# Results of one attention unit and scores of the next in one visit, with the seven products of a step in another order on four banks

## The chip, the cores and the metric

The kernel runs on one core of a Trainium2 chip. The metric is the device time of one execution in microseconds (us), the median of three runs. The engines are TensorE (PE, matrix products; its weight loads are listed as PEld), VectorE (DVE), ScalarE (ACT), GpSimd (POOL) and SyncE (SP, which here only issues DMAs). Products land in PSUM, which has eight banks; a tile of 128 x 512 fp32 fills one. DVE and ACT read PSUM, POOL doesn't.

## The reference, cut to what matters

```python
def reference(q, k, v, moe_w_in, moe_w_out, moe2_w_in, moe2_w_out, moe2_g_ln):
    # retention with a state: batch 4, 8 heads, 768 positions, head size 64
    for t in range(768):
        state = gamma * state + einsum('bhd,bhe->bhde', k[:, :, t], v[:, :, t])
        y[:, :, t] = scale * einsum('bhd,bhde->bhe', q[:, :, t], state)
    x = y.transpose(0, 2, 1, 3).reshape(3072, 512)
    h = x @ moe_w_in                        # 512 -> 2048
    x = (h - tanh(h)) @ moe_w_out           # 2048 -> 512
    h = x @ moe2_w_in                       # 512 -> 1024
    # softmax-weighted h, layer norm with moe2_g_ln, @ moe2_w_out -> 512
```

All is float32. The kernel keeps float32 accuracy by splitting each factor of a large product into a high and a low part and adding three products (high by high, high by low, low by high).

## The kernel before, in words

The attention is cut into units k: 128 positions of one batch, 24 units in all, 16 of them (k = 0 to 15) done in earlier stages. A unit has two parts, both in `unit` (L285). The **scores** (tiles `sc`, 64 small matmuls of 64 x 64 into two banks) are masked on DVE (L337) and make the running states `sb` and `sa` (L342, L345). The **results** (tiles `out`, 64 small matmuls into two banks) use the masked scores and the state; ACT copies a half (L317) and DVE adds the other (L319) into `xf`. `prepare` (L258) scales the input of a unit ahead of its scores, on POOL (L268, L279) and ACT (L275); `load_units` issues the loads of `z`.

The diff touches the stage of **h by seven** (from `ps_h` at L790 to `A.close()`), in which h of the positions 256 to 767 is computed with seven products in place of eight (a Strassen-Winograd scheme). In one step n a block of columns j is treated for a pair p of position blocks: seven products P1 to P7, each of six wide matmuls (128 x 128 by 128 x 512, L818) into one bank. There are 16 steps: n = 0 to 7 for the pair whose input is ready, n = 8 to 15 for the last pair, whose input `xf` comes out of the eight remaining units (k = 16 to 23, called 0 to 7 in `visits`) while steps 0 to 7 run.

Per step: P1(n) goes into bank b1 (`begin`, run in step n - 1) and ACT copies it (`keep`, L828, tile `part`). P2 goes into b3, and DVE adds the copy of P1 (`summed`, L844, tile `hs`). P5 goes into b2 and is copied. P6 is added onto b1 and copied (`u2`). P7 is added onto b1; DVE adds P5's copy. P4 is added onto b1 a step later; P3 is added onto b2 a step later, and DVE adds u2. Four results leave a step through `finish`: tanh on ACT (L834), then h - tanh (L836), on POOL after P2, P3 and P7 and on DVE after P4, then a store `gd` on SP. In steps 1 to 6 a `Factors` object makes the parts of the weights of step n + 1: four sums on DVE (L591 to L594), high parts (`cast`, L610, ACT), low parts (`low`, L614, DVE).

In steps 3 to 8 the input of the last pair is made: `late_x` (`sum_at`, L895 to L901, DVE) subtracts halves of `xf` from each other, and `put_x` (`x_at`) splits one of seven inputs into a high part (L171, ACT, 128 x 1024) and a low part (L172, DVE).

The order: in this stage PE's instructions stand in the order of the code (`manual_schedule`), and `late[0]` is set, so those of ACT, DVE and POOL keep the order of the code among themselves too (`fix`, `pin`). A planner orders only SP's DMAs. Before, the order of the products on PE in a step is P2, P5, P4 (of n - 1), P6, P3 (of n - 1), P1 (of n + 1), P7. `visit(n, m)` is called behind some of the products and runs the scores or the results of a unit there, as `visits` says. The pool `ps_h` has six banks that all of b1, b2 and b3 take in turn; `ps_a` has two banks, for the visits. Behind the stage comes y, the product with the second weights, on four banks from `y_banks`, with the first matmuls of y already in the last step.

Of the kernel before, what the change touches and what calls it, by code (L numbers as in the profile page):

```python
# [26 lines left out]
F32 = mybir.dt.float32  # L27
# [64 lines left out]
def body(ctx: ExitStack, tc, z, w_in, w_out, w_in2, w_out2, g_ln, cst, tab, out):  # L92
# [83 lines left out]
    class Decoder:  # L176
# [24 lines left out]
        def keep(self, fixed=False):  # L201
            while unkept:
                i, wf = unkept.pop(0)
                to = wfd[i % NJ1][:, i // NJ1, :] if i < NF1 else wod[i - NF1]
                eng = nc.gpsimd if i < NF1 else nc.scalar
                pin(eng.dma_start(out=to, in_=wf), fixed)
# [421 lines left out]
    def store_w():  # L628
        while made:
            j, parts_ = made.pop()  # L630
            if j >= NJ1 - 2:
                continue
            for i, u in enumerate(parts_):
                n = 3 if i < 2 else 4
                nc.sync.dma_start(out=wcd[j][i][:, :n, :], in_=u[:, :n, :].bitcast(F32))
# [145 lines left out]
    for b in range(2):  # L781
# [5 lines left out]
    M = ExitStack()  # L787
    M.enter_context(tc.manual_schedule(engines={mybir.EngineType.PE}))
    G = ExitStack()
    ps_h = G.enter_context(tc.tile_pool(name="ps_h", bufs=6, space=PSUM, reuse_waits="tile"))  # L790
    ps_a = G.enter_context(tc.tile_pool(name="ps_a", bufs=2, space=PSUM, reuse_waits="tile"))
    visits = {
        (0, P2): ("sc", 0), (0, P6): ("out", 0), (0, P7): ("sc", 1),
        (1, P5): ("out", 1), (1, P6): ("sc", 2), (1, P7): ("out", 2),
    }
    for k in range(3, 8):
        visits[k - 1, P5] = ("sc", k)
        visits[k - 1, P7] = ("out", k)

    def visit(n, m):  # L800
        if (n, m) not in visits:
            return
        kind, k = visits[n, m]
        k += 4 * B
        if kind == "sc":
            unit(None, k, pool=ps_a)
            load_units(k + 3)
            if k + 1 < NU:
                prepare(k + 1, H // 2, True, False)
        else:  # L810
            unit(k, None, opool=ps_a)

    def product(left, p, m, ph, first=True):
        n = 0
        for i in range(2):
            (ah, al), (xh, xl) = ([t[:, i, :] for t in side] for side in (left[m], xs[p, m]))
            for a, x in ((ah, xh), (ah, xl), (al, xh)):
                nc.tensor.matmul(  # L818
                    ph, a, x, start=first and n == 0, stop=n == 5, skip_group_check=True
                )  # L820
                n += 1

    def bank():
        return ps_h.tile([P, SB], F32, tag="h", name="ph")

    def keep(ph):
        t = t2([P, SB], F32, "part")
# [26 lines left out]
    py = []  # L854

    def y_banks(s):
        at = [(ps_h, "h")] * 4 if s % 2 else [(ps_a, "r"), (ps_a, "r"), (ps_h, "h"), (ps_h, "h")]
        py[:] = [pool.tile([P, SB], F32, tag=tag, name="py") for pool, tag in at]

    def load_g(upto):  # L860
# [19 lines left out]
    def split_wo(f):  # L880
        wo[f] = stage3(wof[f], None, nc.vector, late[0])

    def begin(n):
        b1[n] = bank()
        product(wl[n], q[n][0], P1, b1[n])
        p1[n] = keep(b1[n])

# [16 lines left out]
        (3, P3): P1, (4, P3): P2, (NJ1 - 1, P5): P5, (NJ1 - 1, P6): P6,  # L904
        (NJ1, P2): P7, (NJ1, P6): P4, (NJ1, P7): P3,
    }
    sum_at = {(5, P3): 0, (NJ1 - 1, P2): 1, (NJ1 - 1, P4): 2, (NJ1, P5): 3}

    def after(n, m):
        if (n, m) in sum_at:  # L910
            late_x(sum_at[n, m])
        if (n, m) in x_at:
            at = {P1: (4, 0), P2: (4, 1), P5: (4, 0), P4: (4, 1), P7: (5, 0), P3: (5, 1)}
            t = x_at[n, m]
            if t in at:
                i, h = at[t]
                sums.setdefault(2, {})[t] = xf_of[i][:, h, :, :]
            put_x(2, x_at[n, m], nc.vector)
# [3 lines left out]
    for n in range(len(q) + 1):  # L922
        now, was = n < len(q), n > 0
        p, j = q[n] if now else (NSB, 0)
        if n and len(wq) < NJ1:
            load_wq()
        new = Factors(n + 1) if 1 <= n < NJ1 - 1 else None
        final = n == len(q) - 1

        if n == NJ1 - 1:  # L930
            wl[NJ1] = wl[NJ1 - 1]
            wl[NJ1 + 1] = wl[NJ1 - 2]
        elif NJ1 <= n < len(q) - 2:
            load_wl(n + 2, q[n + 2][1])
        if n == len(q) - 2:
            load_g(4)
            load_wo(3)
        if new:
            new.cast(0)
        if now:  # L940
            b3 = bank()
            product(wl[n], p, P2, b3)
            h = summed(b3, p1.pop(n))
            if new:
                new.low(0)
            finish(2 * p, j, h, nc.gpsimd)
            after(n, P2)
            visit(n, P2)
            b2[n] = bank()
            product(wl[n], p, P5, b2[n])  # L950
            p5[n] = keep(b2[n])
            store_w()
            after(n, P5)
            visit(n, P5)
            if final:
                split_p(0)
        else:
            y_banks(2)
            load_g(5)
            load_wo(4)  # L960
            products_y(0, gp.pop(0), wo[0], py)
        if was:
            pp, jj = q[n - 1]
            product(wl[n - 1], pp, P4, b1[n - 1], False)
            finish(2 * pp, jj + NJ1, b1.pop(n - 1), nc.vector)
            after(n, P4)
        if new:
            new.sums()
        if now:
            product(wl[n], p, P6, b1[n], False)  # L970
            u2[n] = keep(b1[n])
            if new:
                new.cast(1)
            visit(n, P6)
            after(n, P6)
            if new:
                new.cast(2)
            if final:
                split_wo(0)
        else:  # L980
            split_p(2)
            split_wo(2)
        if was:
            product(wl.pop(n - 1), pp, P3, b2[n - 1], False)
            h = summed(b2.pop(n - 1), u2.pop(n - 1))
            if new:
                new.low(1)
                new.low(2)
            finish(2 * pp + 1, jj, h, nc.gpsimd)
            after(n, P3)  # L990
        if now:
            if n + 1 < len(q):
                begin(n + 1)
            if new:
                new.cast(3)
            product(wl[n], p, P7, b1[n], False)
            h = summed(b1[n], p5.pop(n))
            finish(2 * p + 1, j + NJ1, h, nc.gpsimd)
            if final:
                split_p(1)  # L1000
            if new:
                new.low(3)
            visit(n, P7)
            after(n, P7)
            if final:
                split_wo(1)
    A.close()


# [159 lines left out]
    for n, (s, f) in enumerate(steps):  # L1169
        if n:  # L1170
            late[0] = late[0] or s == NSB - 1 and f == 6
            if f == 0:
                y_banks(s)
                if s == NSB - 1:
                    bank_of[:] = [(ps_a, "r"), (ps_a, "r"), (ps_h, "h"), (ps_h, "h")]
            load_g(n + 5)
            load_wo(n + 4)
            while len(gp) < min(3 + late[0], len(steps) - n):
                split_p(n + len(gp))
            if n + 2 < NF1:  # L1180
                split_wo(n + 2)
            products_y(f, gp.pop(n), wo[f], py)
        if f == NF1 - 1:
            keep_y(s, py)
        if s >= NSB - 3 and n % 2 == 0 and com.n[2] < 12:
            com.step()
        if s == NSB - 1:
            if f == 0:
                load_y(0)
            if f == 2:  # L1190
                sum_y(0)
                load_y(1)
            if f == 4:
                split_y(0)
            if f == 6:
                sum_y(1)
            if f == 9:
                load_y(2)
            if f == 7:
                pair = Pair(0)  # L1200
            for m in {7: (P1, P2), 8: (P6, P5), 9: (P7, P4), 10: (P3,)}.get(f, ()):
                pair.part(m)
                if m == P6:
                    split_y(1)
            if f == 10:
                pair.sb.exp()
                pair.sa.weigh()
                pair.sb.weigh()
                pair.sa.center()
                pair.sa.turn()  # L1210
            if f == 11:
                pair.sb.center()
                pair.sb.turn()
                turn(0)
            if f == 12:
                pair.sa.norm()
            if f == 13:
                pair.sb.norm()
            if f == 12:
                sum_y(2)  # L1220
        m = n - 2 * NF1 - 6
        if m >= 0 and m % 3 == 0:
            step2(m // 3)
# [157 lines left out]
```

## Time and profile before

| | us |
|---|---|
| median of 3 runs | 829.03 (828.62 to 829.21) |
| profiled execution | 828.99 |
| its span, first to last instruction | 827.0 |
| PE busy in the span | 813.6 (98%) |
| DVE, ACT, POOL busy | 539.9, 467.7, 281.7 |
| the stage of h by seven in the trace | 229.5 to 406.6 |

The profile is one execution recorded by the hardware profiler; times in it count from the span's start, and 2.0 us of the execution lie outside the span. A timeline lists instructions in order of time with start, duration, engine, line, operation, tiles and shapes; "x64" is 64 instructions merged into one line, and square brackets give the idle time of the engine ahead of it and what ended it. Matmuls overlap: a wide one is listed with 0.39 us, and the next starts 0.227 us behind its start. On ACT and DVE too an instruction is listed some 0.1 us longer than the distance to the next start.

### The profile page before, as it was taken

What the parts mean: (1) busy time and instruction counts of PE and PEld (TensorE: products, weight loads), DVE (VectorE), ACT (ScalarE), POOL (GpSimd) and SP (SyncE); (2) the same over time, 40 slices, a digit from 0 to 9 for tenths busy, and PEclk for the clock granted to TensorE, in tenths of its full rate; (3) what the DMA queues carried; (4) which work ended last, traced back from release to release, by engine and by line L of the source; (5) the groups of instructions that cost most, each with busy time, mean ns of one, the idle gap of its engine ahead of it and who ended that gap; (6) DMA issues with size and microseconds to landing.
All of it is one profiled execution on the core that took longest, in us unless ns stands there. A gap on an engine that the chain in (4) does not pass through costs nothing.

```text
span 827.0 us, 15372 instructions
## 1 busy us (share of the span) xinstructions
PE 813.6 (98%) x5784; PEld 670.0 (81%) x5784; DVE 539.9 (65%) x990; ACT 467.7 (57%) x860; POOL 281.7 (34%) x305
## 2 busy tenths in 40 slices
PE   6999999999999999999999999999999999999997
PEld 5788888888888878888888888888888888888886
DVE  3898866999647776532672978446666566566671
ACT  4466644546456665544561627245777677677772
POOL 4322210040444443434300260152655445555310
PEclk9999999999999999999999999999999999999999
DMA  9996353333869954696593728361877777776694
GB/s 358 408 406 219 110 168 127 127 142 130 336 219 353 368 189 178 244 411 218 202 352 104 266 65 305 119 211 52 204 152 153 154 153 152 153 154 127 128 194 86
DMA packets 167577, 169.42 MB, mean 205 GB/s; under 512 B 105552, under 2 KB 118224, under 8 KB 167504
## 3 DMA queue, kind: packets, MB, share of 16 engines
q1 hardware_dynamic: 160176, 153.51, 61.1%
q10 hardware_dynamic: 6048, 10.74, 3.8%
q0 software_dynamic: 1280, 4.20, 1.3%
q8 instruction: 45, 0.74, 0.4%
q14 instruction: 28, 0.23, 0.1%
HBM read 107.08 MB, written 61.34 MB: 204 GB/s over the span
## 4 chain that ended last, share of the span: by engine, by line
PE 95%; DMA 4%; issue 1%; ACT 0%; SPq 0%; ACTq 0%
PE py L429 32%; PE ph L818 19%; PE po L1110 16%; PE ph L1025 14%; PE ph L404 11%; DMA z<-z 2%; PE out L256 2%; PE sc L256 2%; DMA raw<-w_in 1%; SPq L239 0%; ACT ob L1118 0%; ACT w L160 0%; ACT xh L389 0%; ACTq L1118 0%
## 5 line engine op out<-in xcount | busy, mean ns | idle before, releaser
L429 PE MATMUL py<-gp,w 128*128 128x512 f32 x768 | 175.1, 389 | 0.0
L429 PEld LDWEIGHTS py<-gp,w 128*128 128x128 f32 x768 | 144.1, 188 | 29.9
L1110 PE MATMUL po<-w,uh 128*128 128x512 f32 x384 | 106.5, 389 | 0.0
L836 POOL TENSOR_TENSOR hs<-hs,th 128x512 f32<-128x512 f32 x48 | 62.6, 1309 | 117.5 <-ACT th L834 108.8
L1110 PEld LDWEIGHTS po<-w,uh 128*128 128x128 f32 x384 | 72.1, 188 | 15.0
L404 PE MATMUL ph<-xh,w 128*128 128x512 f32 x256 | 82.3, 395 | 0.8 <-ACT w L160 0.6
L429 PE MATMUL py<-gh,w 128*128 128x512 f32 x256 | 78.9, 389 | 0.0
L160 ACT CAST w<-wf 128x512 fp32r<-128x512 f32 x70 | 43.0, 619 | 51.0 <-DVE wf L150 39.0
L172 DVE TENSOR_TENSOR gp<-g,gp 128x512 fp32r<-128x512 f32 x64 | 49.9, 789 | 25.2 <-ACT gp L171 25.1
L1110 PE MATMUL po<-w,ul 128*128 128x512 f32 x192 | 63.0, 389 | 0.0
L834 ACT ACTIVATE th<-hs 128x512 f32<-128x512 f32 x48 | 30.4, 632 | 52.1 <-DVE hs L844 52.0
L161 DVE TENSOR_TENSOR w<-wf,w 128x512 fp32r<-128x512 f32 x70 | 50.6, 727 | 13.0 <-ACT w L160 11.6
L1025 PE MATMUL ph<-w,yhs 128*128 128x512 f32 x192 | 59.1, 389 | 0.0
L404 PEld LDWEIGHTS ph<-xh,w 128*128 128x128 f32 x256 | 47.9, 188 | 12.5 <-DVE w L161 1.1
L818 PE MATMUL ph<-xh,wch 128*128 128x512 f32 x140 | 56.4, 403 | 0.0
L429 PEld LDWEIGHTS py<-gh,w 128*128 128x128 f32 x256 | 48.0, 188 | 9.9
L818 PE MATMUL ph<-xl,wch 128*128 128x512 f32 x140 | 54.8, 391 | 0.0
L818 PE MATMUL ph<-xh,wcl 128*128 128x512 f32 x140 | 54.7, 390 | 0.0
L171 ACT CAST gp<-g 128x512 fp32r<-128x512 f32 x64 | 38.6, 617 | 27.8 <-DMA g<-gd 19.5
L818 PE MATMUL ph<-xh,wc 128*128 128x512 f32 x168 | 52.6, 389 | 0.0
L844 DVE TENSOR_TENSOR hs<-ph,part 128x512 f32<-128x512 f32 x48 | 32.8, 688 | 30.1 <-PE ph L818 18.3
L1098 DVE TENSOR_TENSOR ul<-hn,uh 128x1024 fp32r<-128x1024 f32 x24 | 31.8, 1325 | 29.3 <-ACT uh L1094 29.3
(133 smaller groups left out, 1719.6 us busy)
## 6 DMA issues: line engine op xcount, KB each, us to landing
z<-z SPq DMA_DIRECT2D x48, 512.0 KB, 8.3
g<-gd SPq DMA_DIRECT2D x64, 256.0 KB, 5.0
raw<-w_in SPq DMA_DIRECT2D x24, 512.0 KB, 8.4
raw<-w_out SPq DMA_DIRECT2D x24, 512.0 KB, 4.0
gd<-hs SPq DMA_DIRECT2D x48, 256.0 KB, 4.5
ud<-ut SPq DMA_DIRECT2D x24, 512.0 KB, 3.0
hn<-ud SPq DMA_DIRECT2D x24, 512.0 KB, 6.9
y1d<-ysb SPq DMA_DIRECT2D x24, 256.0 KB, 3.9
```

The source lines that it names most:

```text
L160: pin(nc.scalar.copy(hi, wf), fixed)
L161: pin(eng.tensor_tensor(lo, wf, hi.bitcast(F32), ALU.subtract), fixed)
L171: fix(nc.scalar.copy(h, src))
L172: fix(eng.tensor_tensor(o, src, h.bitcast(F32), ALU.subtract))
L256: pin(nc.tensor.matmul(o, a, b, start=True, stop=True, skip_group_check=True), held[0])
L404: nc.tensor.matmul(ph, a[:, k, :], x, start=n == 0, stop=n == 3 * NK - 1), s < 2
L429: nc.tensor.matmul(py[e], a[:, cols], x, start=f == 0 and n == 0, stop=f == NF1 - 1 and n == 2)
L818: nc.tensor.matmul(ph, a, x, start=first and n == 0, stop=n == 5, skip_group_check=True)
L836: fix(eng.tensor_tensor(g, h, th, ALU.subtract))
L844: fix(nc.vector.tensor_tensor(h, ph, part, ALU.add))
L1025: nc.tensor.matmul(ph, x[:, r, :], w, start=first and n == 0, stop=n == 5, skip_group_check=True)
L1110: nc.tensor.matmul(po, a[:, f, :], dec2.w[f][lo], start=n == 0, stop=n == len(todo) - 1)
```

## The change

Scores and results share a visit: visit k runs the results of unit k - 1 and then the scores of unit k, so there are nine visits (the first has only scores, the last only results) in place of sixteen. They stand behind P2 and P5 of step 0, P4 and P7 of step 1, and P7 of steps 2 to 6. `ps_a` gets four banks. `ps_h` gets two tags of two banks each: b1 for the bank of P1, P6, P7 and P4, b2 for that of P5 and P3 and that of P2. The order of the products in a step becomes P2, P4 (of n - 1), P3 (of n - 1), P6, P1 (of n + 1), P5, P7. With them move their copies, sums, the weight stores (`store_w`), the parts of the weights, the last subtraction of `late_x` (behind P4 instead of P5 of step 8) and some splits for y. The banks of y and of the last stage's first pair are taken from the new pools.

```diff
--- before.py
+++ after.py
@@ -787,28 +787,23 @@
     M = ExitStack()
     M.enter_context(tc.manual_schedule(engines={mybir.EngineType.PE}))
     G = ExitStack()
-    ps_h = G.enter_context(tc.tile_pool(name="ps_h", bufs=6, space=PSUM, reuse_waits="tile"))
-    ps_a = G.enter_context(tc.tile_pool(name="ps_a", bufs=2, space=PSUM, reuse_waits="tile"))
-    visits = {
-        (0, P2): ("sc", 0), (0, P6): ("out", 0), (0, P7): ("sc", 1),
-        (1, P5): ("out", 1), (1, P6): ("sc", 2), (1, P7): ("out", 2),
-    }
-    for k in range(3, 8):
-        visits[k - 1, P5] = ("sc", k)
-        visits[k - 1, P7] = ("out", k)
+    ps_h = G.enter_context(tc.tile_pool(name="ps_h", bufs=2, space=PSUM, reuse_waits="tile"))
+    ps_a = G.enter_context(tc.tile_pool(name="ps_a", bufs=4, space=PSUM, reuse_waits="tile"))
+    visits = {(0, P2): 0, (0, P5): 1, (1, P4): 2, (1, P7): 3}
+    for k in range(4, 9):
+        visits[k - 2, P7] = k
 
     def visit(n, m):
         if (n, m) not in visits:
             return
-        kind, k = visits[n, m]
-        k += 4 * B
-        if kind == "sc":
+        k = visits[n, m] + 4 * B
+        if k > 4 * B:
+            unit(k - 1, None, opool=ps_a)
+        if k < NU:
             unit(None, k, pool=ps_a)
             load_units(k + 3)
             if k + 1 < NU:
                 prepare(k + 1, H // 2, True, False)
-        else:
-            unit(k, None, opool=ps_a)
 
     def product(left, p, m, ph, first=True):
         n = 0
@@ -820,8 +815,8 @@
                 )
                 n += 1
 
-    def bank():
-        return ps_h.tile([P, SB], F32, tag="h", name="ph")
+    def bank(tag):
+        return ps_h.tile([P, SB], F32, tag=tag, name="ph")
 
     def keep(ph):
         t = t2([P, SB], F32, "part")
@@ -854,7 +849,7 @@
     py = []
 
     def y_banks(s):
-        at = [(ps_h, "h")] * 4 if s % 2 else [(ps_a, "r"), (ps_a, "r"), (ps_h, "h"), (ps_h, "h")]
+        at = [(ps_h, f"b{1 + e % 2}") for e in range(NK)] if s % 2 else [(ps_a, "r")] * NK
         py[:] = [pool.tile([P, SB], F32, tag=tag, name="py") for pool, tag in at]
 
     def load_g(upto):
@@ -881,7 +876,7 @@
         wo[f] = stage3(wof[f], None, nc.vector, late[0])
 
     def begin(n):
-        b1[n] = bank()
+        b1[n] = bank("b1")
         product(wl[n], q[n][0], P1, b1[n])
         p1[n] = keep(b1[n])
 
@@ -904,7 +899,7 @@
         (3, P3): P1, (4, P3): P2, (NJ1 - 1, P5): P5, (NJ1 - 1, P6): P6,
         (NJ1, P2): P7, (NJ1, P6): P4, (NJ1, P7): P3,
     }
-    sum_at = {(5, P3): 0, (NJ1 - 1, P2): 1, (NJ1 - 1, P4): 2, (NJ1, P5): 3}
+    sum_at = {(5, P3): 0, (NJ1 - 1, P2): 1, (NJ1 - 1, P4): 2, (NJ1, P4): 3}
 
     def after(n, m):
         if (n, m) in sum_at:
@@ -938,7 +933,7 @@
         if new:
             new.cast(0)
         if now:
-            b3 = bank()
+            b3 = bank("b2")
             product(wl[n], p, P2, b3)
             h = summed(b3, p1.pop(n))
             if new:
@@ -946,14 +941,6 @@
             finish(2 * p, j, h, nc.gpsimd)
             after(n, P2)
             visit(n, P2)
-            b2[n] = bank()
-            product(wl[n], p, P5, b2[n])
-            p5[n] = keep(b2[n])
-            store_w()
-            after(n, P5)
-            visit(n, P5)
-            if final:
-                split_p(0)
         else:
             y_banks(2)
             load_g(5)
@@ -964,35 +951,40 @@
             product(wl[n - 1], pp, P4, b1[n - 1], False)
             finish(2 * pp, jj + NJ1, b1.pop(n - 1), nc.vector)
             after(n, P4)
+            visit(n, P4)
         if new:
             new.sums()
-        if now:
-            product(wl[n], p, P6, b1[n], False)
-            u2[n] = keep(b1[n])
-            if new:
-                new.cast(1)
-            visit(n, P6)
-            after(n, P6)
-            if new:
-                new.cast(2)
-            if final:
-                split_wo(0)
-        else:
-            split_p(2)
-            split_wo(2)
+            new.cast(1)
         if was:
             product(wl.pop(n - 1), pp, P3, b2[n - 1], False)
             h = summed(b2.pop(n - 1), u2.pop(n - 1))
             if new:
                 new.low(1)
-                new.low(2)
             finish(2 * pp + 1, jj, h, nc.gpsimd)
             after(n, P3)
         if now:
+            product(wl[n], p, P6, b1[n], False)
+            u2[n] = keep(b1[n])
+            if new:
+                new.cast(2)
+                if not was:
+                    new.low(1)
+            visit(n, P6)
+            after(n, P6)
+            if final:
+                split_wo(0)
+                split_p(0)
             if n + 1 < len(q):
                 begin(n + 1)
             if new:
+                new.low(2)
                 new.cast(3)
+            b2[n] = bank("b2")
+            product(wl[n], p, P5, b2[n])
+            p5[n] = keep(b2[n])
+            store_w()
+            after(n, P5)
+            visit(n, P5)
             product(wl[n], p, P7, b1[n], False)
             h = summed(b1[n], p5.pop(n))
             finish(2 * p + 1, j + NJ1, h, nc.gpsimd)
@@ -1004,6 +996,9 @@
             after(n, P7)
             if final:
                 split_wo(1)
+        else:
+            split_p(2)
+            split_wo(2)
     A.close()
 
 
@@ -1172,7 +1167,7 @@
             if f == 0:
                 y_banks(s)
                 if s == NSB - 1:
-                    bank_of[:] = [(ps_a, "r"), (ps_a, "r"), (ps_h, "h"), (ps_h, "h")]
+                    bank_of[:] = [(ps_a, "r")] * 4
             load_g(n + 5)
             load_wo(n + 4)
             while len(gp) < min(3 + late[0], len(steps) - n):
```

## Rows read from the trace of the kernel before

**Rows 1.** The page's first part: busy us, share of the span, instructions.
```profile
PE 813.6 (98%) x5784; PEld 670.0 (81%) x5784; DVE 539.9 (65%) x990; ACT 467.7 (57%) x860; POOL 281.7 (34%) x305
```

**Rows 2.** Busy time by stretch; steps 2, 6, 8, 9, each P2 to P2.
```profile
core 0: us, PE busy (x) PEld busy (x) DVE busy (x) ACT busy (x) POOL busy (x), PEclk, DMA share, GB/s
254.94:267.10 12.16, 12.16 (x176) 9.78 (x171) 8.44 (x19) 7.58 (x18) 5.70 (x5) 1.00 1.00 356
...
303.70:316.21 12.51, 12.49 (x177) 9.99 (x171) 9.38 (x20) 6.71 (x14) 3.89 (x3) 1.00 0.24 89
...
325.86:335.38 9.52, 9.52 (x43) 7.88 (x42) 6.73 (x8) 5.83 (x9) 3.82 (x3) 1.00 0.64 242
335.38:345.33 9.95, 9.95 (x43) 7.73 (x42) 5.46 (x7) 5.34 (x10) 3.85 (x3) 1.00 0.59 185
```

**Rows 3.** Timeline of DVE and PE around the scores in step 6.
```profile
306.10 0.75 DVE L319 TENSOR_TENSOR xf<-xf,out 128x256 f32<-128x256 f32 x2 [0.64 <-ACT xf L317]
...
306.65 1.50 PE L256 MATMUL sc<-vq,z 64*64 64x64 f32 x64
```

**Rows 4.** Timeline of PE in P3 of step 8.
```profile
341.05 0.50 PE L818 MATMUL ph<-xl,wch 128*128 128x512 f32 x1
341.38 0.39 PE L818 MATMUL ph<-xh,wcl 128*128 128x512 f32 x1
```

**Rows 5.** Timeline of PE around the first visit of the stage (scores alone).
```profile
231.97 0.39 PE L818 MATMUL ph<-xh,wcl 128*128 128x512 f32 x1
232.29 1.16 PE L256 MATMUL sc<-vq,z 64*64 64x64 f32 x64
233.38 0.50 PE L818 MATMUL ph<-xh,wch 128*128 128x512 f32 x1
233.72 0.39 PE L818 MATMUL ph<-xl,wch 128*128 128x512 f32 x1
```

**Rows 6.** Timeline of PE around a joint visit in an earlier stage.
```profile
65.02 0.39 PE L404 MATMUL ph<-xh,w 128*128 128x512 f32 x1
65.34 0.34 PE L256 MATMUL out<-qs,sa 64*64 64x64 f32 x8
...
66.32 0.66 PE L256 MATMUL sc<-qs,z 64*64 64x64 f32 x32
...
67.38 0.50 PE L404 MATMUL ph<-xh,w 128*128 128x512 f32 x1
```

**Rows 7.** Timeline of DVE in steps 7 to 9.
```profile
317.96 0.69 DVE L844 TENSOR_TENSOR hs<-ph,part 128x512 f32<-128x512 f32 x1
318.57 1.41 DVE L895 TENSOR_TENSOR xf<-xf 128x512 f32<-128x512 f32 x2
320.87 1.34 DVE L172 TENSOR_TENSOR xl<-xf,xh 128x1024 fp32r<-128x1024 f32 x1 [0.90 <-ACT xh L171]
...
326.21 1.28 DVE L844 TENSOR_TENSOR hs<-ph,part 128x512 f32<-128x512 f32 x2
...
339.25 1.74 DVE L172 TENSOR_TENSOR xl<-xf,xh 128x1024 fp32r<-128x1024 f32 x1 [2.04 <-ACT xh L171]
```

**Rows 8.** Timeline of ACT at the start of step 8.
```profile
326.93 0.63 ACT L834 ACTIVATE th<-hs 128x512 f32<-128x512 f32 x1 [1.89 <-DVE hs L844]
327.46 0.57 ACT L828 COPY part<-ph 128x512 f32<-128x512 f32 x1
```

**Rows 9.** Timeline of DVE (sums, sum of P3) and ACT (high part) in step 4.
```profile
286.33 0.53 DVE L591 TENSOR_TENSOR wsum<-wq 128x256 f32<-128x256 f32 x1
...
287.91 0.68 DVE L844 TENSOR_TENSOR hs<-ph,part 128x512 f32<-128x512 f32 x1
...
289.22 1.03 ACT L171 CAST xh<-xf 128x1024 fp32r<-128x1024 f32 x1
```

**Rows 10.** Timeline of POOL and DVE at the first subtractions of halves, step 5.
```profile
301.70 1.29 POOL L836 TENSOR_TENSOR hs<-hs,th 128x512 f32<-128x512 f32 x1 [2.82 <-ACT th L834]
...
301.74 2.52 DVE L895 TENSOR_TENSOR xf<-xf 128x512 f32<-128x512 f32 x2
```

**Rows 11.** Timeline of SP at one load of a unit; the page's DMA part.
```profile
257.19 1.56 SPq L239 DMA_DIRECT2D z<-z  x2
...
z<-z SPq DMA_DIRECT2D x48, 512.0 KB, 8.3
```

## Prediction

> **What bounds the kernel now.** I read the busy times first, then the stage's stretches step by step, then TensorE's timeline at the visits, then the queues of VectorE (DVE) and ScalarE (ACT) in the steps where new input is split. TensorE (PE) is busy 98% of the span [rows 1], so time changes only by what PE executes or waits for. The stretches of [rows 2] run from the P2 of one step to the P2 of the next. A step without a visit (8) takes 9.52 us: 42 matmuls, 0.227 us each, 1.36 us per product. A step with two visits (2) takes 12.16 us. Step 6 takes 12.51 and step 9 takes 9.95, so PE already waits 0.35 and 0.43 us there. For step 6 the place is the scores at 306.65, which end 0.3 us late: they take the bank pair that the DVE addition at 306.10 was reading until 306.85 [rows 3]. For step 9 it is P3(8), whose second matmul at 341.05 needs the low part of its input that DVE finished at 340.99 [rows 4, 7]; restarting costs 0.11 us beyond the wait (0.33 to the next start where 0.227 is usual) [rows 4]. P3(8) is thus at its limit before the change; keep that in mind.
>
> **What the change takes away.** A lone visit: last wide matmul at 231.97, next wide one at 233.38, and that one holds its successor 0.34 us [rows 5]. That is 1.41 + 0.34 - 2 x 0.227 = 1.30 us. The same 128 small matmuls in one visit are seen in the stage before (results of one unit, scores of the next): from 65.02 to 67.38, 2.36 us [rows 6], and with the same 0.34 behind it 2.25 us. One joint visit saves 2 x 1.30 - 2.25 = 0.35 us. Sixteen visits become nine, seven of them joint: 2.4 us; I take 2.5, since a few matmuls behind each switch are slower too. The bank wait of step 6 goes as well, because a visit gets four banks that were last used a step earlier: 0.35 us. The 0.43 us of step 9 is replaced by what follows.
>
> **What the order costs.** PE's order per step was P2 P5 P4 P6 P3 P1 P7 and becomes P2 P4 P3 P6 P1 P5 P7 (P4 and P3 belong to the step before). With two banks per tag instead of six in turn, four waits become tight, counted in products that lie between: P4(n-1) adds onto the bank that DVE sums after P7(n-1), with two products between them before and one now (1.36 us, plus a visit ahead of steps 2 to 7); P3(n-1) has four products between itself and P7(n-1) before and two now, which counts where its input is split behind that P7; P1(n+1) takes the bank that the subtraction after P4(n-1) frees, with two products between; P5(n) takes the bank of the sum after P3(n-1), with two between. A sum starts 0.25 us behind its product (P2(7) of the trace ends at 316.21 + 1.36 + 0.14 for the visit, its sum starts at 317.96 [rows 2, 7]), takes 0.6 to the next start (two in 1.28 at 326.21 [rows 7]) and needs about 0.1 to release PE: 0.95 us behind P7, so steps 10 to 15, with nothing else queued, fit in 1.36. ACT and DVE run in program order: the copy after P1(8) starts at 327.46, right behind a tanh at 326.93 that waited for DVE's sum at 326.21 [rows 7, 8], though step 8 had begun on PE at 325.86 [rows 2]. So every late instruction delays all behind it, and I line the queues up.
>
> Steps 3 and 4 (a half of late input is split behind P3). From the end of P4(n-1): tanh 0.63 [rows 8] with its start and hand-over 0.9, subtraction 0.6 (as long as a sum), the four sums 1.58 (286.33 to 287.91), the sum of P3 and its tanh 1.3, the copy of 1024 columns 0.95 (289.22, 1.03 long), the copy of P6 0.6: 5.9 to 6.0 us [rows 9]. P7(n) writes that bank and stands four products, 5.44 us, behind: 0.4 to 0.6 us of wait each. Before, the split stood behind the copy of P6. Two waits of 0.5 and two restarts: 1.25 us.
>
> Steps 7 to 9 (four more splits, and subtractions on their inputs). Take the end of P2(7) as zero. DVE: sum to 0.85; two subtractions, 1.41 long, to 2.2; the subtraction of P4(6) to 2.85; the subtraction of 1024 columns, about 1.2 like the low parts, held back by GpSimd's own operation for P2 (POOL, 1.3 us, itself held to 2.2 by the two subtractions), to 4.5; the sum of P3(6) to 5.1. ACT: tanh to 5.8; copy of P6(7) to 6.3; high part for P6 to 7.2; copies of P1(8) and P5(7) to 8.2; high part for P5 to 9.2. DVE: its low part, 1.26, to 10.4; only then the sum of P7(7), to 11.0 [rows 7 to 9]. P4(7) wants to start after seven products, at 9.52: about 1.4 us of wait. Carried on in the same way: P1(9) waits 0.7 (the subtraction of P4(7) queues behind the low part for P7), P5(8) 0.3, P3(8) 1.2 (the low part for P3). That is 3.6 us and four restarts, 4.05 us.
>
> A check on it from below: in the trace DVE goes from the sum at 317.96 to the end of the low part for P3 at 340.99 [rows 7], 23.0 us, with PE's P3(8) the eighteenth product behind P2(7) and just late. The same instructions lie between after the change, but P3(8) is the sixteenth. If the queues take the same 23.0 us, PE loses 2 x 1.36 = 2.7 us, plus 0.1. So steps 7 to 9 cost 2.8 to 4.1 us unless the new order lets ACT and DVE run faster; I take 4.05, since the waits on the way are themselves queued.
>
> The hold by POOL is seen at 301.74: two subtractions take 2.52 us beside a POOL operation started at 301.70, and 1.41 us at 318.57 with POOL idle at the start [rows 7, 10]. The Trainium skill (SBUF — State Buffer, Who interferes with whom) says that a DVE instruction with two SBUF inputs and a reading GpSimd instruction exclude each other, first come first served. The 1.1 us lost agrees with full exclusion over 1.25 us of overlap. Had they merely shared, the wait at P4(7) would be about 0.2 us shorter, which the range covers.
>
> **Other edits.** The halves of the results' last splits (f = 2) move behind P3(15), whose tanh stands ahead of them: ready about 3.4 us after P3(15) where the third matmul of y's step 2 wants them at 3.2; between 0 and 0.4, I take 0.2. The weight stores move behind P5, three products later on SP's queue: nothing is reloaded before step 8, so nothing, or under 1 us if a buffer that they hold is wanted. The low piece of the second half moves behind P1(n+1): its reader is a step away. The y banks of both pools have been idle for over a step: nothing. Results wait for the masked scores a whole step: nothing.
>
> **Sum.** -2.5 - 0.35 - 0.43 + 1.25 + 4.05 + 0.2 = +2.2 us on the profiled execution's 828.99, so 831.2; that execution lies 0.04 below the median 829.03, which I neglect. A measurement of this kernel can tell about 0.2% (1.7 us) from no change: faster is below 827.4, slower above 830.7.
>
> **Rivals.** (a) The queues catch up: the new order spreads ACT's and DVE's work better, and the waits are a small part of what I count. For it: DVE is busy 6.73 of 9.52 us in step 8 [rows 2], so there is idle time to win. Its place is the chain to P4(7): it decides where DVE's sum of P7(7) ends within 0.4 us of P2(8) instead of 1.4, as the later waits grow out of this one. Against it: that idle time is ACT and DVE waiting for each other in turn, which the new order keeps. With no wait 828.99 - 3.3 = 825.7; with a third of the 5.5 us 827.5. Chance 0.2. (b) Only the bound from below holds in steps 7 to 9 and steps 3 and 4 lose half: -3.3 + 2.8 + 0.6 gives 829.1. Chance 0.2. (c) A late input load, a loss beyond the forecast. The load for unit 20 is issued at the joint visit behind P4 of step 1, and its scaling stands on ACT and POOL at the visit behind P7, five products and one visit (9.0 us) later. An issue of a pair takes 1.56 us and a landing 8.3 in the median [rows 11], 9.9 in all; the queues bear about 1 us beyond the visit; from there each further us blocks ACT and reaches PE in full, since the copies that free P7 and P5's banks stand behind. It decides when the load lands over 1 us after that visit's end; 2 us later it gives 833.2. Chance 0.1.
>
> **How the numbers follow.** The forecast, 831.2, has a chance of 0.5 and a range of its own of 829.8 to 832.6, from 4.1 to 6.9 us of waits and restarts; 0.43 of it lies above 830.7 and 0.07 below. With (c) slower holds 0.53, with (b) no change 0.27, and (a) gives faster 0.2. The range runs from 826.5, which takes in half of (a), to 833.2, the 2 us of (c).
>
> **What would show it.** Right: nine visits of L256 in the PE timeline, seven of them 2.25 us; a gap of 1 to 1.5 us ahead of P4 of step 8, released by DVE's sum (L844), smaller ones ahead of P1, P5 and P3 of steps 8 and 9, and 0.4 to 0.6 us ahead of P7 in steps 3 and 4, released by ACT's copy (L828). Steps 10 to 15 stay at 9.52 us. Wrong: steps 7 to 9 together near 28.6 us, or gaps at the visits released by a load or by POOL.

## The result, and the profile after

The changed kernel takes 834.6 us (median of 6 runs, 834.06 to 835.09) where the kernel before, run beside it, takes 829.08 (828.62 to 829.52): 1.0068 times as long, 95% interval 1.0058 to 1.0078. It is slower, as forecast, but by 5.5 us instead of 2.2, and 1.4 us above the range given. The profiled execution has a span of 832.4 us, 5.4 more than before.

The page's first part, which answers [rows 1]: TensorE is busy for as long as before.

```profile
PE 813.6 (98%) x5784; PEld 669.2 (80%) x5784; DVE 539.9 (65%) x990; ACT 466.2 (56%) x860; POOL 287.0 (34%) x305
```

The span less the busy time is 18.8 us where it was 13.4: all of the 5.4 us are idle time of PE. The stretches from P2 to P2, as in [rows 2]; steps 3, 4 and 5, then 7 to 10 of the changed kernel:

```profile
core 0: us, PE busy (x) PEld busy (x) DVE busy (x) ACT busy (x) POOL busy (x), PEclk, DMA share, GB/s
266.96:279.80 12.84, 12.06 (x177) 9.69 (x170) 9.77 (x18) 8.04 (x19) 5.63 (x6) 1.00 1.04 377
279.80:292.31 12.51, 12.06 (x177) 9.69 (x170) 9.76 (x18) 8.16 (x20) 5.75 (x6) 1.00 0.94 363
292.31:304.09 11.78, 11.78 (x178) 9.77 (x171) 10.45 (x19) 7.38 (x20) 5.93 (x6) 1.00 0.52 187
...
314.93:324.58 9.65, 9.65 (x48) 7.99 (x43) 6.84 (x10) 5.19 (x11) 4.32 (x3) 1.00 0.24 89
324.58:336.93 12.35, 10.33 (x44) 7.65 (x42) 7.78 (x9) 6.29 (x11) 3.85 (x3) 1.00 0.65 231
336.93:348.16 11.23, 10.22 (x43) 7.68 (x42) 4.62 (x6) 5.34 (x9) 3.87 (x3) 1.00 0.92 313
348.16:357.68 9.52, 9.52 (x43) 7.88 (x42) 2.77 (x4) 4.19 (x7) 3.83 (x3) 1.00 1.03 413
```

The granted clock is 1.00 throughout. Step 5, a joint visit and nothing waited for, takes 11.78 us where two visits took 12.16; steps 3 and 4 take 1.06 and 0.73 more than step 5. P2(7) starts at 314.93, 1.28 us earlier than before (316.21): up to there the change wins. Steps 7 to 9 then take 33.24 us (314.93 to 348.16, rounded) where they took 29.13. Steps 10 to 15 stay at 9.52.

Read as a ledger of TensorE's starts, with the forecast beside it. The first line is the 1.28 us above plus the waits of the second line.

| term | forecast, us | measured, us |
|---|---|---|
| joint visits and the bank wait of step 6 | -2.85 | -3.05 |
| waits of P7 in steps 3 and 4, with restarts | +1.25 | +1.77 |
| steps 7 to 9 (with the 0.43 that goes) | +3.62 | +4.11 |
| y, splits behind P3(15) | +0.2 | +1.13 |
| y, banks handed to the last stage | 0 | +1.06 |
| behind the last matmul | 0 | +0.3 |
| sum | +2.2 | +5.3 |

The gain is where it was expected. TensorE's timeline at one joint visit (wide matmuls are L813 now; lines behind the stage's head lie five lower than before):

```profile
252.72 0.39 PE L813 MATMUL ph<-xh,wcl 128*128 128x512 f32 x1
253.03 0.34 PE L256 MATMUL out<-vq,sa 64*64 64x64 f32 x8
...
254.02 1.13 PE L256 MATMUL sc<-vq,z 64*64 64x64 f32 x64
255.08 0.50 PE L813 MATMUL ph<-xh,wch 128*128 128x512 f32 x1
255.41 0.39 PE L813 MATMUL ph<-xl,wch 128*128 128x512 f32 x1
```

From 252.72 to 255.08 it is 2.36 us, the figure of [rows 6], and the next start is 0.33 behind. Reckoned as in the prediction, the seven joint visits take 2.23 or 2.24 us each.

**Step 3.** ACT and DVE ahead of the wait of P7(3), then PE:

```profile
268.59 0.41 DVE L342 TENSOR_TENSOR sb<-sa,sc 128x256 f32<-128x256 f32 x1
268.92 0.69 DVE L839 TENSOR_TENSOR hs<-ph,part 128x512 f32<-128x512 f32 x1
269.98 0.63 ACT L829 ACTIVATE th<-hs 128x512 f32<-128x512 f32 x1 [1.28 <-DVE hs L839]
270.52 0.58 ACT L829 ACTIVATE th<-ph 128x512 f32<-128x512 f32 x1
271.74 0.59 DVE L591 TENSOR_TENSOR wsum<-wq 128x256 f32<-128x256 f32 x1
...
273.37 0.68 DVE L839 TENSOR_TENSOR hs<-ph,part 128x512 f32<-128x512 f32 x1
274.09 0.63 ACT L829 ACTIVATE th<-hs 128x512 f32<-128x512 f32 x1 [2.70 <-DVE hs L839]
274.63 1.03 ACT L171 CAST xh<-xf 128x1024 fp32r<-128x1024 f32 x1
275.56 0.58 ACT L823 COPY part<-ph 128x512 f32<-128x512 f32 x1
276.19 0.50 PE L813 MATMUL ph<-xh,wch 128*128 128x512 f32 x1 [0.78 <-ACT part L823]
```

The chain is the forecast's, link by link: tanh behind P4 (270.52), four sums from 271.74, the sum of P3 (273.37), its tanh, the copy of 1024 columns, the copy of P6, and P7 starts when that ends. It begins late: P2(3) starts at 266.96, P4(2) ends two products and a restart later at 269.8, but ACT takes that product's tanh at 270.52, behind the tanh of P2. The sum for that one had to wait on DVE for the joint visit's work (268.59) and starts at 268.92, half a us behind P2's end; to the tanh it is another 1.06 us, where 0.72 is usual (273.37 to 274.09). P7(3) starts 1.165 us behind the matmul ahead of it, a wait of 0.94 with 0.227 taken off (the brackets count from the listed end of a matmul and read less); P7(4) waits 0.61.

**Steps 7 to 9.** DVE and ACT, and the three largest waits of PE, in order of time:

```profile
324.48 1.07 ACT L171 CAST xh<-xf 128x1024 fp32r<-128x1024 f32 x1
...
325.58 1.23 DVE L172 TENSOR_TENSOR xl<-xf,xh 128x1024 fp32r<-128x1024 f32 x1 [0.70 <-ACT xh L171]
326.72 1.28 DVE L839 TENSOR_TENSOR hs<-ph,part 128x512 f32<-128x512 f32 x2
327.46 0.50 PE L813 MATMUL ph<-xh,wch 128*128 128x512 f32 x1 [1.36 <-DVE hs L839]
...
329.70 2.14 DVE L172 TENSOR_TENSOR xl<-xf,xh 128x1024 fp32r<-128x1024 f32 x1 [1.70 <-ACT xh L171]
331.77 0.68 DVE L831 TENSOR_TENSOR th<-ph,th 128x512 f32<-128x512 f32 x1
332.50 0.50 PE L813 MATMUL ph<-xh,wch 128*128 128x512 f32 x1 [0.66 <-DVE th L831]
...
339.82 1.48 DVE L172 TENSOR_TENSOR xl<-xf,xh 128x1024 fp32r<-128x1024 f32 x1 [1.64 <-ACT xh L171]
341.36 0.50 PE L813 MATMUL ph<-xl,wch 128*128 128x512 f32 x1 [1.01 <-DVE xl L172]
```

P4(7) at 327.46 starts as soon as the first of the two sums from 326.72 is done. That sum stood behind the low part for P5 (325.58), and that behind its high part on ACT (324.48). By starts the waits are 1.52 at P4(7), 0.82 at P1(9) and 1.28 at P3(8), where 1.4, 0.7 and 1.2 were forecast; P5(8) doesn't wait, P7(8) does for 0.08. A low part of 1024 columns takes 1.23 us at 325.58 and 2.14 at 329.70, beside a subtraction of POOL. The queue behind P2(7), which ends at 316.43, ran as the prediction lined it up, link by link within 0.15 us, as far as DVE's sum of P7(7).

**y, step 2.** Behind the stage (its last wide matmul starts at 409.16):

```profile
410.37 0.63 ACT L829 ACTIVATE th<-hs 128x512 f32<-128x512 f32 x1 [1.49 <-DVE hs L839]
410.90 0.61 ACT L171 CAST gp<-g 128x512 fp32r<-128x512 f32 x1
411.08 1.29 POOL L831 TENSOR_TENSOR hs<-hs,th 128x512 f32<-128x512 f32 x1 [4.17 <-ACT th L829]
411.55 1.37 DVE L172 TENSOR_TENSOR gp<-g,gp 128x512 fp32r<-128x512 f32 x1 [1.27 <-ACT gp L171]
412.84 0.68 DVE L161 TENSOR_TENSOR w<-wf,w 128x512 fp32r<-128x512 f32 x1
412.98 2.24 PE L429 MATMUL py<-gp,w 128*128 128x512 f32 x7 [0.39 <-DVE gp L172]
```

**The start of the last stage:**

```profile
591.60 0.69 DVE L437 COPY ysb<-py 128x512 f32<-128x512 f32 x1 [0.67 <-PE py L429]
592.35 0.74 PE L1020 MATMUL ph<-w,yha 128*128 128x512 f32 x2 [0.78 <-DVE ysb L437]
```

The last y matmul starts at 591.18; the first product of the last stage waits for a copy of a y bank. In the kernel before, the same step passes at the usual pitch of 0.227 us (its last y matmul starts at 587.22):

```profile
587.44 0.61 PE L1025 MATMUL ph<-w,yha 128*128 128x512 f32 x2
```

### The profile page after: what moved, and what is told of

The parts are those of the page before. It is cut to its first block, busy times and chain, and to the rows that moved or that the text cites. A ratio compares the mean times of both kernels' runs of the same rounds, so it can differ in the third digit from the quotient of the medians.

```text
span 832.4 us, 15359 instructions
## 1 busy us (share of the span) xinstructions
PE 813.6 (98%) x5784; PEld 669.2 (80%) x5784; DVE 539.9 (65%) x990; ACT 466.2 (56%) x860; POOL 287.0 (34%) x305
## 4 chain that ended last, share of the span: by engine, by line
PE 86%; DMA 5%; issue 3%; DVE 2%; ACT 2%; POOL 1%; SPq 0%; POOLq 0%; DVEq 0%; ACTq 0%
PE py L429 31%; PE po L1105 16%; PE ph L1020 14%; PE ph L813 12%; PE ph L404 10%; DMA z<-z 2%; PE out L256 2%; PE sc L256 1%; DMA raw<-w_in 1%; DMA gd<-hs 1%; DVE hs L839 1%; POOL hs L831 1%; ACT part L823 1%; ACT th L829 1%; ACT xh L171 0%
## 5 line engine op out<-in xcount | busy, mean ns | idle before, releaser
L172 DVE TENSOR_TENSOR gp<-g,gp 128x512 fp32r<-128x512 f32 x64 | 47.6, 752 | 26.4 <-ACT gp L171 26.3
L813 PE MATMUL ph<-xh,wch 128*128 128x512 f32 x140 | 56.3, 402 | 3.2 <-DVE hs L839 1.4
L813 PE MATMUL ph<-xl,wch 128*128 128x512 f32 x140 | 54.7, 391 | 1.0 <-DVE xl L172 1.0
L813 PE MATMUL ph<-xh,wcl 128*128 128x512 f32 x140 | 54.7, 391 | 0.0
L813 PE MATMUL ph<-xh,wc 128*128 128x512 f32 x168 | 52.4, 389 | 0.0
```

The lines of the kernel that those rows point to most:

```text
L172: fix(eng.tensor_tensor(o, src, h.bitcast(F32), ALU.subtract))
L813: nc.tensor.matmul(ph, a, x, start=first and n == 0, stop=n == 5, skip_group_check=True)
```

## Experiments

Two theories stand against each other in most of them. The theory of the prediction: ACT and DVE work as one chain in program order, and a wait of PE comes from how many products lie between an instruction and the product that needs it. The rivals: two banks per tag are the cause, or a single misplaced split, or the load of a joint visit on DVE. Times are medians, and each ratio is to the kernel before, run beside it.

**e1_split: the last split of y ahead of P3(15) again.**

```diff
+        if not now:
+            split_p(2)
+            split_wo(2)
         if was:
             product(wl.pop(n - 1), pp, P3, b2[n - 1], False)
 ...
-        else:
-            split_p(2)
-            split_wo(2)
```

> The last splits for y (f = 2) go back ahead of P3 of step 15; all else is the changed kernel. Theory (they stand on ACT behind the tanh of P3, and y's step 2 waits for them): the gaps of 0.65, 0.38 and 0.11 us on PE at 413 go, the time falls by 1.1 us to about 833.5. Rival (y's step 2 waits for a load of g or of the weights, and the splits only look late): no change, 834.6.

Measured 833.53 us, 1.0057 (1.0041 to 1.0072); the span is 831.1 instead of 832.4. The waits near 413 are gone and nothing takes their place. The 1.1 us belong to this one move.

**e2_pools: the pools opened in the other order.**

```diff
-    ps_h = G.enter_context(tc.tile_pool(name="ps_h", bufs=2, ...
     ps_a = G.enter_context(tc.tile_pool(name="ps_a", bufs=4, ...
+    ps_h = G.enter_context(tc.tile_pool(name="ps_h", bufs=2, ...
```

> The two pools of four banks are opened in the other order, so that the last y's banks lie at the other end of PSUM; all else is the changed kernel. Theory (the pools of the last stage lie over the banks of the two old ones, and its first product falls on a bank of the last y that is still being copied out): the gap of 0.95 us on PE at 592 goes, the time falls by 1.1 us to about 833.5. Rival (the first product waits for its input, or any four banks of y collide): the gap stays, 834.6.

Measured 833.08 us, 1.0050 (1.0036 to 1.0064), span 831.3. The wait at 592 is gone, 1.07 us by TensorE's starts. Which physical banks the last step of y holds decides it: with the pools as changed, it holds banks that the last stage's first product is given.

**e3_old7: old order from step 7 on.** Steps 0 to 6 as changed; from step 7 the body of the kernel before (its order, copies, sums and splits), with b3 from the now idle visit banks.

```diff
+        if n < NJ1 - 1:
             ... (the changed step)
+        else:
+            b3 = ps_a.tile([P, SB], F32, tag="r", name="ph")
+            ... (the step of before)
```

> From step 7 on the products, copies, sums and splits go back to the old order, with the bank of P2 taken from the visits' pool, idle by then; joint visits and the new order stay in steps 0 to 6, and P1, P6, P7, P4 keep two banks. Theory (waits of steps 7 to 9 come from the chain of ACT and DVE to the split inputs, which the new order wants two products earlier): steps 7 to 9 fall from 33.2 us to the 29.1 of before, and the gaps at 413 go too since the last step has the old order: 5.2 us less, about 829.4. Rival (two banks for P1, P6, P7 and P4 are too few): P1 of step 9 still waits about 0.8 us, and no more than 3 us are won, 831.5.

Measured 831.64 us, 1.0031 (1.0019 to 1.0042): 3.0 us back, 2.2 short of what was expected. Steps 7 to 9 take 31.0 us (33.2 as changed, 29.1 before), and the waits near 413 are gone, since the splits stand in their old place too. What remains is one long wait, of P1(9), and a small one of P1(10). DVE and PE at P1(9):

```profile
329.35 2.06 DVE L172 TENSOR_TENSOR xl<-xf,xh 128x1024 fp32r<-128x1024 f32 x1 [1.69 <-ACT xh L171]
...
332.46 0.68 DVE L831 TENSOR_TENSOR th<-ph,th 128x512 f32<-128x512 f32 x1
333.20 0.50 PE L813 MATMUL ph<-xh,wch 128*128 128x512 f32 x1 [1.50 <-DVE th L831]
```

P1(9) takes the bank that the subtraction behind P4(7) frees, and that stands behind a low part. In this order two banks are a cause, as the rival had it.

**e4_put6: the splits of steps 3 and 4 behind P6.**

```diff
-        (3, P3): P1, (4, P3): P2,
+        (3, P6): P1, (4, P6): P2,
```

> In steps 3 and 4 the split of a half of late input moves from behind P3 to behind P6, past the copy of P6; all else is the changed kernel. Rival (the gaps ahead of P7 of steps 3 and 4 are a matter of place alone): the gaps of 0.94 and 0.61 us go with their restarts, 1.8 us less, 832.8. Theory (DVE has no room in steps with a visit, and the split pushes what follows): the gap moves to P5 of the steps 4 and 5, which take the bank of the sum of P3, 0.65 us each; the time stays within 0.6 us of 834.6.

Measured 835.34 us, 1.0077 (1.0064 to 1.0089), 0.7 more than the changed kernel, a little beyond the 0.6 expected. P7(3) no longer waits; P1(5) waits 0.26, P7(4) 0.46, P1(6) 0.20 and P7(5) 0.43, each with a restart. That is 1.8 us in all, as much as before the move, so the rest of the 0.7 isn't in these waits. The wait moves on, though to P1 and P7 of the next steps and not to P5.

**e5_banks: more banks in the changed order, steps 8 to 11.**

```diff
-        b1[n] = bank("b1")
+        b1[n] = ps_a.tile([P, SB], F32, tag="r", name="ph") if NJ1 <= n < 12 else bank("b1")
 ...
-            b3 = bank("b2")
+            b3 = bank("b1" if NJ1 <= n < 12 else "b2")
```

> New order throughout, but in steps 8 to 11 more banks: P1 (with P6, P7, P4) of those steps from the visits' pool, P2 on the tag left free by it, so that no product there waits for a bank. Theory (in the new order the split of P3's input ends the wait whatever the banks): the gap of 0.82 us ahead of P1 of step 9 goes, but P7 of step 8 and P3 of step 8 wait that much longer, time stays at 834.6 within 0.3. Rival (bank waits add up): the gap's 0.82 and 0.11 us are won, 833.6.

Measured 834.01 us, 1.0061 (1.0048 to 1.0075), span 832.0 against 832.4. P1(9) doesn't wait any more, P7(8) waits 1.03 us in its stead, and P3(8) waits as before:

```profile
335.04 0.50 PE L813 MATMUL ph<-xh,wch 128*128 128x512 f32 x1 [0.87 <-ACT part L823]
...
340.96 0.50 PE L813 MATMUL ph<-xl,wch 128*128 128x512 f32 x1 [1.01 <-DVE xl L172]
```

Steps 7 to 9 take 33.18 us, where the changed kernel takes 33.24; the rest of the 0.6 us by which the median is lower, more than the 0.3 expected, isn't in these steps. In the changed order banks alone don't help: the chain of ACT and DVE is what is late, and PE meets it at the next place.

**e6_apart: new order and four banks, but results and scores apart,** results behind P5, scores behind P7.

```diff
     for k in range(4, 9):
-        visits[k - 2, P7] = k
+        visits[k - 2, P5] = ("out", k - 1)
+        visits[k - 2, P7] = ("sc", k)
```

(The first two steps' visits are parted in the same way, and one more stands behind P1(1).)

> The changed kernel with results and scores in visits of their own again: from step 2 on results behind P5 and scores behind P7, in steps 0 and 1 likewise one or two products apart; four banks for the visits and the new order stay. Theory: seven more pairs of switches on PE, 0.35 us each, add 2.4 to 2.6 us, 837.1, and the waits of steps 3 and 4 change little since DVE's work in a step is the same. Rival (a joint visit saves PE time but gives it back, since it loads DVE in one piece ahead of P2): the waits of steps 3 and 4 fall by about 1 us, 836.

Measured 839.65 us, 1.0128 (1.0114 to 1.0142), 5.0 more than the changed kernel. Seven switches more explain 2.5 of it (7 x 0.35), and that is all that was expected. The rest is mostly in waits: P4(7) grows to 1.87 us, and new ones come ahead of P4(6), 0.26, and P1(8), 0.70. In steps 3 and 4 the two waits trade places, P7(3) 0.43 us and P7(4) 1.10, and their sum stays at 1.5. So parting the visits doesn't remove the waits of steps 3 and 4, as the rival had it, and it adds later ones. How much a joint visit's work on DVE adds to any one wait, this run doesn't show, since the visits also moved on PE.

**e7_p5late: the split of P5 behind P7 of step 7,** so that the sum ahead of P4(7) comes first.

```diff
-(NJ1 - 1, P5): P5,
+(NJ1 - 1, P7): P5,
```

> The changed kernel with one split moved: the input of P5 is split behind P7 of step 7, past DVE's sum of P7, instead of ahead of it. Theory (one chain of ACT and DVE instructions, whose length decides): the wait of 1.5 us ahead of P4 of step 8 goes, and comes back ahead of P1 of step 9, which then waits 2.8 us instead of 0.8; the time is 834.6 to 835.3. Rival (the split stands in a bad place, and that wait starts the others): 1.5 us and more are won, 833 or less.

Measured 836.9 us, 1.0088 (1.0072 to 1.0103), 2.3 more than the changed kernel. P4(7) doesn't wait, as expected, but P1(9) waits 3.03 us, where 2.8 was expected, and P3(8) still 1.28. What comes behind the long wait wasn't expected at all (last section): it costs the profiled execution of 837.47 us another 2.8, without which it would lie at 834.7, in the range expected.

**e9_three: as e3_old7, with a third bank where P1(9) and P1(12) start.**

```diff
-        b1[n] = bank("b1")
+        b1[n] = ps_a.tile([P, SB], F32, tag="r", name="ph") if n in (9, 12) else bank("b1")
```

> As the run with the old order from step 7 on, but P1 of the steps 9 and 12 goes into a bank of the visits' pool, so that P1, P6, P7, P4 have three banks in turn. Theory (there P1 of step 9 waited 1.66 us for the subtraction behind P4 of step 7 only because it took that bank): that wait and the 0.35 us one a step later go, steps 7 to 9 take 29.1 us as before the change, about 829.4. Rival (the queues of ACT and DVE end later than before the change): the wait moves to P3 of step 8, 831.

Measured 829.15 us, 1.0003 (0.9994 to 1.0012). Steps 7 to 9 take 29.1 us, as before the change. So the 4.1 us of these steps take both to give back: the old order (2.2) and a third bank (1.9).

**e10_all: e9_three with e2_pools, and the splits of steps 3 and 4 behind P5 with their low parts on POOL.**

```diff
-        (3, P3): P1, (4, P3): P2,
+        (3, P5): P1, (4, P5): P2,
 ...
-put_x(2, x_at[n, m], nc.vector)
+put_x(2, x_at[n, m], nc.gpsimd if n < 5 else nc.vector)
```

> The run with the old order from step 7 on and three banks, with the pools opened in the other order, and with the splits of steps 3 and 4 moved behind P5 and their low parts given to POOL. Theory: no wait at 592 (1.1 us), none in steps 3 and 4 (1.8 us, since neither the copy of P6 nor DVE's sums stand behind the split), joint visits keep their 2.5 us: 826.5, 2.5 us faster than the kernel before. Rival (POOL, 2.5 us longer in those steps, holds DVE off SBUF, and the waits return on P5 or P1): 828 or more.

Measured 829.05 us, 1.0000 (0.9992 to 1.0009): no gain, where 826.5 was expected. P7(3) is free, but P7(4) waits 1.02 us and P7(5) 1.13: the waits return, as the rival had it, though on P7 and not on P5 or P1. POOL's queue and one of DVE's sums:

```profile
277.82 2.56 POOL L172 TENSOR_TENSOR xl<-xf,xh 128x1024 fp32r<-128x1024 f32 x1 [2.13 <-ACT xh L171]
280.33 1.30 POOL L831 TENSOR_TENSOR hs<-hs,th 128x512 f32<-128x512 f32 x1
281.58 1.76 POOL L268 TENSOR_TENSOR vq<-z,tab 128x512 f32<-128x512 f32 x1
283.28 0.81 POOL L279 TENSOR_TENSOR vq<-z,con 128x256 f32<-128x256 f32 x1
284.06 1.47 POOL L831 TENSOR_TENSOR hs<-hs,th 128x512 f32<-128x512 f32 x1
...
284.30 1.51 DVE L593 TENSOR_TENSOR wsum<-wq 128x256 f32<-128x256 f32 x1
...
287.93 0.51 PE L813 MATMUL ph<-xh,wch 128*128 128x512 f32 x1 [0.86 <-ACT part L823]
```

POOL is at work without a break from 277.8 to 285.5, and a sum of 256 columns that takes 0.41 us at 285.73 takes 1.51 beside it. The split's place and its engine were changed together, so the run doesn't show what either would do alone.

**e11_keep: e10_all without the moved splits** (joint visits and new order in steps 0 to 6, old order from step 7, a third bank for P1(9) and P1(12), pools in the other order).

> Joint visits and the new order in steps 0 to 6, the old order from step 7 on with three banks for P1, P6, P7 and P4, and the pools opened in the other order; the splits of steps 3 and 4 stay behind P3. Theory: as the run with three banks, 829.15, less the 1.1 us of the gap at 592: 828.0, 0.1% faster than the kernel before; the waits of steps 3 and 4 stay, 1.8 us. Rival (the copies of the last y delay another product once that gap is gone): 829.

Measured 827.96 us, 0.9985 (0.9976 to 0.9993) of the kernel before: it beats both kernels, the one before by 0.15%. Steps 7 to 9 of it, from P2(7) to P2(10), take 29.1 us, as before the change:

```profile
314.86:343.96 29.10, 29.10 (x132) 23.53 (x127) 19.14 (x23) 16.40 (x28) 10.68 (x8) 1.00 0.55 187
```

What is left of the losses are the waits of P7(3) and P7(4), 0.67 and 0.62 us.

## Why the sign was right and the size wrong

The gain was right, and so were the places of the waits in the stage, but for P5(8), and what ends them. The sum failed in four terms, all too small: the y banks (put at nothing), the splits behind P3(15), steps 3 and 4, and steps 7 to 9. The first two make up 2.0 of the 3.2 us.

**The joint visits** and the bank wait of step 6: right, 3.05 us for 2.85. The price of a joint visit, taken from another stage [rows 6], held to 0.02 us.

**Steps 3 and 4**: the mechanism was right and the term too small, 1.77 us for 1.25. The step that failed is "from the end of P4(n-1)": it took ACT as free there. In step 3 it came to that tanh some 0.5 us late: a quarter of a us because the sum of P2 stood on DVE behind the last work of the joint visit, work that I had left out of the queues I lined up, and 0.3 because the hand-over of that sum to ACT took longer than usual, for which the trace shows no reason. It isn't chance: it takes 1.05 or 1.06 us in each of the seven kernels that have the joint visits and open the pools in this order, and 0.71 or 0.72 in the three that open them in the other (e2_pools, e10_all, e11_keep). Why the order of the pools matters here stays open.

**Steps 7 to 9**: right in place, order and releaser, and slightly small: P4(7) 1.52 for 1.4, P1(9) 0.82 for 0.7, P3(8) 1.28 for 1.2, P5(8) nothing for 0.3; in all 4.11 for 3.62. The bound from below (2.8, rival b) was far too low: the queues took 24.6 us in the new order (from DVE's sum for P2(7) at 316.69 to the end of the low part for P3 at 341.30), not the same 23.0. One reading was wrong, without effect on the sum: of the 0.43 us that step 9 lost before the change, P3(8) caused only the restart of 0.11, and most of the rest stood ahead of P7(9), 0.15 us of wait and a restart of 0.11, released by a copy on ACT. Its first matmul in the kernel before:

```profile
343.82 0.50 PE L818 MATMUL ph<-xh,wch 128*128 128x512 f32 x1
```

Rival (a), that ACT and DVE catch up, fell altogether. That in the new order the waits come from ACT and DVE, bound by each other in turn, and not from banks, is shown by e5_banks, where the wait moved on, and by e7_p5late, where one split moved a product later only moved the wait; in the old order, though, e3_old7 shows the bank of P1(9) as a cause of its own, 1.9 us, which the prediction counted only as a wait that is queued behind others.

The argument "steps 10 to 15 fit in 1.36" held: 9.52 us each.

**The splits behind P3(15)**: 1.13 us for 0.2. I had them ready 3.4 us behind P3(15) and wanted at 3.2. The trace has P3(15) end at 409.4, the first low part ready at 412.9 and the second at 413.5, 3.5 and 4.1 us behind it. A low part of 512 columns takes 0.68 us where POOL is idle (as at 412.84) and the first one took 1.37, since POOL's own subtraction for P3(15) started 0.47 us ahead of it. The prediction counts such a hold in step 7 and names none here. The Trainium skill (SBUF — State Buffer, Who interferes with whom) says that a DVE instruction with two SBUF inputs and a reading GpSimd instruction exclude each other; 411.08 + 1.29 = 412.37 for POOL and 1.37 instead of 0.68 for DVE agree with that, and so do the 1.51 us of e10_all.

**"The y banks of both pools have been idle for over a step: nothing."** This is the step that was plainly wrong, 1.06 us of wait and restart. I followed the banks at the start of y, where it holds, and not at its end, where the pools are closed and the last stage opens its own over the same banks. e2_pools takes the wait away by nothing but the order in which two pools are opened.

**The rest**, 0.3 us, lies behind the last matmul: from the start of the last stage on, each matmul starts 5.09 us later than before, up to the last one, and the span ends 5.38 later. What lengthens the end was not followed up. **Rival (c)**, a late load of unit 20, did not come: every wait of PE over 0.2 us in this stage is released by DVE or ACT.

Together the misses are 0.5 + 0.5 + 0.9 + 1.1 + 0.3 = 3.3 us, less 0.2 of better visits, against the 3.2 by which the span missed the forecast. All of these misses lie on the same side. The range had been built from rivals that make the stage itself cheaper or one load late; it held nothing for small terms, put at nothing or nearly so, that are all wrong upwards.

## What to carry to other kernels

Joining two visits of small matmuls pays what an existing joint one shows, but a reorder of products has to be counted in products between each instruction of the helpers and the product that needs it; where two helpers hand work to each other, as here in the changed order, moving one split or adding one bank moved the wait and didn't remove it. When pools are changed, follow each bank beyond the stage, up to the first product that takes it in the next one. And where an edit hurts only some steps, keep it in the others: joint visits in steps 0 to 6, with the old order and a third bank from step 7 and the pools in the other order, gave 0.15% where the whole change lost 0.68%.

## What the runs showed of the hardware beyond that

In e7_p5late the wait of P1(9) had TensorE idle for 2.87 us, and behind it the granted clock is 0.50, which is 1.2 GHz of 2.4. The timeline of PE, and two stretches (columns as above):

```profile
333.05 0.80 PE L813 MATMUL ph<-xh,wch 128*128 128x512 f32 x1 [2.87 <-DVE th L831]
```

```profile
333.05:339.00 5.95, 5.95 (x14) 4.69 (x15) 2.91 (x3) 2.96 (x5) 1.29 (x1) 0.50 0.25 90
339.20:342.00 2.80, 2.80 (x14) 2.31 (x13) 0.69 (x1) 0.84 (x2) 0.13 (x1) 1.00 0.89 241
```

From 333.65 to 338.8 the matmuls start 0.427 us apart instead of 0.227, and at 339.1 the clock is back: 12 x 0.2 us and the two ends, 2.8 us lost. The Trainium skill (TensorE: Matmul & The Clock Gate, Wait — 56ns, not 53.3ns?) gives 426.7 ns for 512 columns at 1.2 GHz, which agrees. The waits of the changed kernel, 1.36 us idle at most in this stage, left the clock at 1.00. So the price of a wait isn't proportional to its length: this one cost nearly twice its own. The loss isn't the same each time: this execution and one more have a mean granted clock of 0.995 and take 837.47 and 837.7 us, and the other two have 0.998 and take 836.09 and 836.33.
